# A second order for every queue of a gated recurrence and gated linear unit kernel

## The chip, the core and the metric

The kernel runs on one core of one Trainium2 chip. The metric is the device time of one execution in microseconds, as the median over several runs. A profile is one execution of its own: it has a span, from the first to the last instruction, and a time a little longer than the span.

## The reference

The inputs are `x`, `r_gate` and `i_gate`, each 4 x 6336 x 256 in fp32, a vector `a_param` of 256, two 256 x 256 matrices and the weights of a causal convolution with five taps per channel.

```python
a_base = sigmoid(a_param)
a_t  = exp(8 * sigmoid(r_gate) * log(clip(a_base)))
norm = sqrt(max(1 - a_t * a_t, 1e-6))
u    = norm * sigmoid(i_gate) * x
h[t] = a_t[t] * h[t-1] + u[t]              # y = all h, per batch and channel
gate = sigmoid(causal_conv5(y, conv_w))    # depthwise
out  = (gate * (y @ w_val)) @ w_out
```

## The kernel before

The 4 x 6336 rows are laid end to end and cut into 51 windows of 512 rows, but for windows 0, 1 and 50, which have 256. A window is the unit of loads, gates, convolutions, products and stores. Windows are put together to 28 chunks: chunks 0, 1 and 2 are windows 0, 1 and 2, chunks 3 to 25 have two windows each, chunks 26 and 27 are windows 49 and 50. A chunk is the unit of squares, of the norm, and of the scan along time, whose result each next scan of the same half of channels needs. Twelve batches of chunks share one square root each (`BATCHES`), and one or two chunks share an exponential (`GROUPS`).

There is no scheduler at work: the kernel is under manual scheduling, and one string, `ORDER`, holds every step as a word. A loop goes through the words and emits each step's instructions, so the string fixes the order of the instructions on every engine and on the DMA queue. A word has the form `name.index.index@banks`: `cv.5@0,1` is the convolution of window 5 into PSUM banks 0 and 1; `sc.3.1` is the scan of chunk 3 for the second half of the channels. Each engine takes its own steps in the order of the string, and semaphores make a step wait for its inputs, and for whoever still reads the buffer or the PSUM bank that it writes.

The steps, with engine and line:

| word | engine | what it does | line |
|---|---|---|---|
| `lr` `li` `lx` | SP queue | load a window of r, i, x (512 KB each) | L274 |
| `st` | SP queue | store a window | L493 |
| `th` | ACT | tanh of half of r and i, for the two sigmoids | L289 |
| `pp` `up` | POOL | 1 + tanh; its product with x | L297, L309 |
| `xp` `uv` | PE, DVE | the same product for six windows, with x copied into PSUM by PE | L314, L323 |
| `tr` `ex` | PE, ACT | transpose the r gate into PSUM; exponential to a | L334, L350 |
| `sq` or `sa` | POOL or ACT | square of a | L358, L366 |
| `rt` | ACT | square root for the norm, in its own function table | L377 |
| `nt` `xg` | PE, DVE | transpose the norm; multiply it into u | L392, L399 |
| `xt` `sc` | PE, DVE | transpose u; scan along time | L408, L430 |
| `cv` `tg` | PE, ACT | convolution by five taps; tanh of its half | L442, L449 |
| `vl` `gv` | PE, DVE | product with `w_val`; gate times value | L457, L462 |
| `ou` | PE | product with `w_out` | L472 |
| `cd` or `ca` | DVE or ACT | copy the output from PSUM | L480, L482 |

The table of ACT functions is switched (L509) whenever a word needs the other table: `rt` has one, `th`, `tg` and `ex` share another. Squares and copies use no table of their own, so they can stand between. `s_small`, `s_ident`, `s_kt`, `s_diag`, `s_wl` and `s_wcast` set up constants and weights.

Buffers are rings that are shared by windows: four windows of r and i (`NRI`), four of x (`NX`), three of gates (`NTRI`), three of conv gates (`NTG`), four of outputs (`NOSB`). A load of window w + 4 can start when the gate step of window w has read its slot, and the SP queue, being in order, holds all that stands behind a load or store that waits. All eight PSUM banks are one tile, and each PE step names the banks that it writes.

Of the kernel before, what the change touches and what calls it, by code (L numbers as in the profile page):

```python
# [42 lines left out]
gv.0 ou.0.0@4 cd.0.0 st.0 sc.4.1 lx.15 cv.3@6,7 th.12 li.16 li.18 tr.7.1@4,5 tg.2 vl.2@2,3 gv.2 tg.3 ex.7.1 sq.6.1
sq.6.0 lx.14 pp.14 pp.12 up.12 tr.7.0@6,7 ex.7.0 sq.7.0 lx.16 cv.4@2,3 tg.4 th.15 ou.2.0@4,5 cd.2.0 sc.4.0 st.2 lr.18
lr.16 vl.3@6,7 xp.13@2,3 vl.4@4,5 gv.4 sq.7.1 rt.4 uv.13 th.16 sq.8.1 sq.8.0 pp.15 up.15 li.17 lr.17 up.14 ou.4.0@4,5
li.19 cv.5@0,1 lr.19 gv.3 cd.4.0 lx.17 tg.5 ou.3.0@6,7 lx.18 st.4 cd.3.0 st.3 nt.5@4,5 li.20 xg.5 pp.16 up.16 th.17
pp.17 lr.20 nt.7@6,7 xg.7 lx.19 li.21 nt.6@2,3 xg.6 th.18 pp.18 lr.21 xt.5@4,5 sc.5.1 up.17 vl.5@6,7 cv.6@0,1 tg.6
th.19 tr.9.1@2,3 ex.9.1 li.22 lr.22 up.18 sq.9.1 pp.19 gv.5 sc.5.0 tr.9.0@6,7 ex.9.0 lx.20 ou.5.0@0,1 cd.5.0 sq.10.1
xt.6@5,4 up.19 sc.6.1 cv.7@0,1 tg.7 cv.8@2,3 th.20 lr.24 tg.8 sc.6.0 vl.6@6,7 gv.6 xt.7@0,1 cv.9@4,5 ou.6.0@6,7 sc.7.0
th.21 tg.9 cd.6.0 vl.7@2,3 gv.7 vl.9@6,7 th.22 tr.11.0@0 sc.7.1 ou.7.0@2,3 vl.8@4,5 sq.9.0 tr.12.0@1 gv.9 ou.9.0@6,7  # L50
gv.8 ou.8.0@4,5 sq.10.0 st.5 cd.7.0 cd.9.0 lx.22 st.6 rt.5 lx.21 nt.8@6,7 lr.23 li.23 cd.8.0 nt.9@4,5 pp.22 pp.21
up.22 pp.20 up.20 up.21 xg.8 ex.12.0 xg.9 ex.11.0 li.24 st.7 st.9 li.25 lr.25 lx.23 lx.24 li.26 lr.26 th.23 xt.8@6,7
sc.8.0 sq.11.0 pp.23 sq.12.0 lr.27 li.27 cv.11@2,3 tg.11 cv.10@4,5 sc.8.1 cv.12@0,1 st.8 th.24 pp.24 tg.10 tg.12
vl.11@2,3 tr.11.1@6 ex.11.1 gv.11 vl.10@4,5 gv.10 th.25 xt.9@0,1 sc.9.0 tr.12.1@2 ex.12.1 ou.11.0@6,7 cd.11.0
# [24 lines left out]
lx.42 up.42 st.30 cv.33@0,1 li.45 vl.33@4,5 tg.33 st.32 gv.33 nt.21@6,7 th.44 nt.20@0,1 xg.20 lx.45 lr.47 li.48 lr.48
th.46 pp.44 xg.21 nt.22@2,3 xg.22 lx.44 cv.35@4,5 th.45 pp.45 pp.46 up.45 st.31 li.47 ou.33.0@0,1 ca.33.0 tg.35  # L80
xt.20@6,7 sc.20.0 tr.23.1@2,3 ex.23.1 sc.20.1 cv.34@0,1 tg.34 cv.36@4,5 sq.24.1 tg.36 vl.35@2,3 gv.35 vl.36@0,1 gv.36
tr.23.0@6,7 vl.34@2,3 gv.34 ou.35.0@4,5 cd.35.0 lx.46 st.33 up.44 xt.21@0,1 sq.23.1 th.48 pp.48 ex.23.0 sq.24.0
sc.21.0 sc.21.1 th.47 cv.38@2,3 tg.38 ou.36.0@4,5 ou.34.0@6,7 ca.36.0 sq.23.0 ca.34.0 xt.22@2,3 tr.25.0@0 ex.25.0
sc.22.1 sq.25.0 tr.25.1@4 ex.25.1 sc.22.0 cv.37@6,7 tg.37 cv.39@0,1 tg.39 vl.40@4,5 vl.38@6,7 gv.38 sq.25.1 rt.10
st.35 li.49 st.36 vl.37@0,1 st.34 vl.39@2,3 lx.49 lr.49 lr.50 lx.48 gv.37 ou.38.0@6,7 cd.38.0 st.38 gv.39 cv.40@0,1
ou.37.0@6,7 cd.37.0 st.37 lx.47 nt.23@2,3 nt.24@6,7 tg.40 up.46 th.49 ou.39.0@0,1 ca.39.0 xg.23 xt.23@2,3 xg.24
cv.41@6,7 gv.40 ou.40.0@0,1 tg.41 ca.40.0 pp.49 pp.47 sc.23.1 cv.42@4,5 vl.41@0,1 sc.23.0 tg.42 gv.41 tr.26.0@3 li.50
ex.26.0 vl.42@6,7 st.39 up.47 th.50 xt.24@4,5 nt.25@2,3 gv.42 up.48 xg.25 st.40 ou.41.0@0,1 ca.41.0 st.41 cv.43@6,7
tg.43 vl.43@0,1 tr.27.0@2 tr.26.1@3 ex.26.1 ex.27.0 sc.24.0 gv.43 sc.24.1 ou.42.0@6,7 sa.27.0 ca.42.0 lx.50 st.42
xt.25@4,3 sc.25.0 tr.27.1@2 sq.26.1 ex.27.1 ou.43.0@0,1 ca.43.0 sq.27.1 st.43 cv.44@6,7 tg.44 sc.25.1 cv.45@0,1 tg.45  # L90
# [450 lines left out]
```

## Time and profile before

| what | value |
|---|---|
| median of three runs | 302.48 us (301.65, 302.48, 303.43) |
| profiled execution, its time | 300.32 us |
| its span | 298.5 us |
| what lies around the span | 1.8 us |
| granted clock of TensorE, mean | 0.977 |
| busy: ACT, DVE, PE, POOL | 278.8, 247.6, 246.4, 232.8 us |
| DMA | 104.75 MB, mean 351 GB/s |

Busy time is the union of an engine's instructions. A row of a group of instructions gives the mean duration of one; neighbours on an engine overlap by some 0.1 us, so the spacing of two instructions is a little less than their duration. These are the rows of the groups that the text below uses (duration of one, largest form): gate tanh 1.918 us, exponential of 2048 columns 2.075, conv tanh 1.036, root of 6144 columns 5.329, table load 1.283, copy on ACT 1.020 and on DVE 1.210, scan of 1024 steps 2.335, gate times value 1.209, square on POOL 1.896, product with x on POOL 2.157 after 1.045 for its sum.

### The profile page before, as it was taken

The page shows a single profiled execution, that of the slowest core. Times are in us where ns is not written, and L with a number is a line of the kernel's source. Part 1 is how long each engine was busy: PE and PEld are TensorE (multiplying, and loading weights), DVE is VectorE, ACT ScalarE, POOL GpSimd, SP SyncE. Part 2 cuts the span into 40 slices and gives each one's busy share as a digit, 9 for nine tenths or more (in the row PEclk, how much of TensorE's full clock was granted, in tenths as well). Part 3 has the DMA queues.
Part 4 walks back from the last instruction along what each step waited for, and adds up shares of the span by engine and source line. Part 5 has one row for each costly group of instructions (what it writes and reads, how often), then busy time and mean ns, then how long its engine had stood idle before and what let it go on. Part 6 is the DMA issues. An engine that isn't in the chain of part 4 may idle for free.

```text
span 298.5 us, 6286 instructions
## 1 busy us (share of the span) xinstructions
PE 246.4 (83%) x2509; PEld 167.8 (56%) x2509; DVE 247.6 (83%) x206; ACT 278.8 (93%) x197; POOL 232.8 (78%) x155
## 2 busy tenths in 40 slices
PE   0374577897888598989898899998979999899993
PEld 0134255454556466757664758567647675666662
DVE  2030288849999889999999999999999899899993
ACT  6799999999999999999999999999999999969863
POOL 1478958989999899899999879998995996255300
PEclk9997599999999979999999999999999999999999
DMA  6999999999999999999999998999999977726046
GB/s 252 408 408 385 379 411 407 406 414 406 337 379 370 419 416 415 411 406 321 417 411 375 388 417 335 396 353 361 349 409 419 408 278 270 273 116 248 29 186 246
DMA packets 29995, 104.75 MB, mean 351 GB/s; under 512 B 3335, under 2 KB 3854, under 8 KB 29966
## 3 DMA queue, kind: packets, MB, share of 16 engines
q1 hardware_dynamic: 29952, 104.35, 90.5%
q8 instruction: 19, 0.31, 0.4%
q14 instruction: 10, 0.08, 0.1%
q10 hardware_dynamic: 14, 0.01, 0.0%
HBM read 78.39 MB, written 25.95 MB: 350 GB/s over the span
## 4 chain that ended last, share of the span: by engine, by line
ACT 31%; PE 23%; DVE 13%; issue 13%; DMA 12%; POOL 5%; SPq 1%; ACTq 0%; DVEq 0%; POOLq 0%
ACT tring L289 10%; ACT aring L350 8%; DMA riring<-in_r_gate_dram 7%; DVE yring L430 7%; PE banks L442 5%; ACT tgring L449 5%; PE banks L457 5%; ACT ering L377 4%; PE banks L472 4%; PE banks L392 3%; DMA riring<-in_i_gate_dram 3%; DVE tgring L462 3%; DVE oring L480 2%; DMA xring<-in_x_dram 2%; ACT L509 2%
## 5 line engine op out<-in xcount | busy, mean ns | idle before, releaser
L430 DVE TENSOR_TENSOR_SCAN yring<-aring,yring,banks 128x1024 bf16<-128x1024 f32 (+5 forms) x54 | 106.2, 1988 | 0.9 <-PE banks L408 0.6
L358 POOL TENSOR_TENSOR ering<-aring 128x1024 f32<-128x1024 f32 (+2 forms) x54 | 91.5, 1713 | 9.7 <-ACT aring L350 9.7
L309 POOL TENSOR_TENSOR uring<-tring,xring 128x1024 bf16<-128x1024 bf16 (+1 forms) x45 | 94.6, 2113 | 4.9 <-DMA xring<-in_x_dram 3.5
L289 ACT ACTIVATE tring<-riring 128x2048 bf16<-128x2048 f32 (+1 forms) x51 | 93.8, 1867 | 4.1 <-DMA riring<-in_i_gate_dram 1.9
L297 POOL TENSOR_SCALAR tring<-tring 128x1024 bf16<-128x1024 bf16 (+1 forms) x45 | 45.8, 1026 | 30.5 <-ACT tring L289 30.4
L442 PE MATMUL banks<-yring,diag 64*64 64x512 bf16 (+7 forms) x1080 | 61.9, 361 | 4.6 <-ACT aring L350 1.6
L462 DVE SCALAR_TENSOR_TENSOR tgring<-tgring,banks 128x1024 bf16<-128x1024 bf16 (+1 forms) x51 | 58.9, 1178 | 5.5 <-PE banks L457 4.4
L472 PE MATMUL banks<-wo,tgring 128*128 128x256 bf16 x396 | 51.4, 274 | 4.7 <-DVE tgring L462 3.5
L350 ACT ACTIVATE aring<-banks,khf 128x2048 f32<-128x2048 bf16 (+3 forms) x38 | 54.1, 1474 | 0.5 <-PE banks L334 0.4
L449 ACT ACTIVATE tgring<-banks 128x1024 bf16<-128x1024 f32 (+1 forms) x51 | 50.4, 1009 | 3.4 <-PE banks L442 3.3
L457 PE MATMUL banks<-yring,wv 128*128 128x512 bf16 (+4 forms) x216 | 49.4, 361 | 5.0 <-DVE oring L480 2.2
L472 PEld LDWEIGHTS <-tgring 128*128 128x128 bf16 x396 | 41.0, 114 | 15.7 <-DVE tgring L462 9.6
L442 PEld LDWEIGHTS <-diag 64*64 64x64 bf16 x1080 | 30.3, 106 | 28.8 <-issue 13.6
L377 ACT ACTIVATE ering<-ering 128x4096 bf16<-128x4096 f32 (+5 forms) x15 | 44.9, 3019 | 0.1
L399 DVE TENSOR_TENSOR uring<-banks,uring 128x2048 bf16<-128x2048 bf16 (+2 forms) x28 | 29.8, 1095 | 18.2 <-PE banks L392 17.9
L480 DVE COPY oring<-banks 128x1024 f32<-128x1024 f32 (+1 forms) x35 | 40.6, 1181 | 4.8 <-ACT aring L350 2.4
L334 PE MATMUL banks<-ident_b,tring 128*128 128x128 bf16 x396 | 29.0, 227 | 12.2 <-ACT tring L289 10.4
L334 PEld LDWEIGHTS <-tring 128*128 128x128 bf16 x396 | 25.1, 101 | 17.7 <-ACT tring L289 11.7
L457 PEld LDWEIGHTS <-wv 128*128 128x128 bf16 x216 | 19.7, 97 | 26.3 <-issue 12.4
L392 PE MATMUL banks<-ident,ering 128*128 128x128 f32 x198 | 28.8, 296 | 6.8 <-DVE oring L480 2.6
L392 PEld LDWEIGHTS banks<-ident,ering 128*128 128x128 f32 x198 | 25.9, 208 | 13.5 <-ACT ering L377 7.7
L408 PE MATMUL banks<-ident,uring 128*128 128x128 f32 x198 | 27.5, 282 | 2.6 <-DVE uring L399 2.5
(36 smaller groups left out, 113.1 us busy)
## 6 DMA issues: line engine op xcount, KB each, us to landing
riring<-in_i_gate_dram SPq DMA_DIRECT2D x48, 512.0 KB, 8.2
riring<-in_r_gate_dram SPq DMA_DIRECT2D x48, 512.0 KB, 8.3
xring<-in_x_dram SPq DMA_DIRECT2D x48, 512.0 KB, 8.0
out_dram<-oring SPq DMA_DIRECT2D x48, 512.0 KB, 5.7
riring<-in_r_gate_dram SPq DMA_DIRECT2D x3, 256.0 KB, 6.3
riring<-in_i_gate_dram SPq DMA_DIRECT2D x3, 256.0 KB, 6.5
xring<-in_x_dram SPq DMA_DIRECT2D x3, 256.0 KB, 5.3
out_dram<-oring SPq DMA_DIRECT2D x3, 256.0 KB, 7.3
```

What stands on the lines that cost most here:

```text
L289: nc.scalar.activation(out=tring[:, w % NTRI, a:a + 2, 0:J, :], in_=riring[:, w % NRI, :, 0:J, :], func=ACT.Tanh, scale=0.5)
L309: nc.gpsimd.tensor_tensor(out=u, in0=t1, in1=xt, op=ALU.mult)
L350: nc.scalar.activation(out=dst, in_=src, func=ACT.Exp, scale=khf[:, h:h + 1], bias=khf[:, h:h + 1])
L358: nc.gpsimd.tensor_tensor(out=e, in0=a, in1=a, op=ALU.mult)
L377: nc.scalar.activation(out=ering[:].bitcast(BF16)[:, 4 * o:4 * o + 2 * n], in_=ering[:, 2 * o:2 * o + 2 * n], func=ACT.Sqrt, scale=-0.25, ...
L392: nc.tensor.transpose(out=bank[:, k:k + P], in_=ering[:, e + q:e + wins[w] // 2:nq], identity=ident[:])
L430: nc.vector.tensor_tensor_scan(out=yring[:, h, col:col + o1 - o0], data0=aring[:, h, a_at[c] + o0:a_at[c] + o1], data1=xT[:, o0:o1], initi ...
L442: nc.tensor.matmul(out=gp[oh * 64:oh * 64 + 64, h, a:b], lhsT=diag[half * 64:half * 64 + 64, h, k, :], rhs=yring[half * 64:half * 64 + 64, ...
L449: nc.scalar.activation(out=tgring[:, w % NTG, :, 0:wins[w]], in_=live.pop(("gp", w))[:, :, 0:wins[w]], func=ACT.Tanh, scale=0.5)
L457: nc.tensor.matmul(out=val[:, m, a:b], lhsT=wv[:, hk, m * P:(m + 1) * P], rhs=yring[:, hk, col:col + b - a], start=(hk == 0), stop=(hk == ...
L462: nc.vector.scalar_tensor_tensor(out=tgring[:, w % NTG, :, 0:wins[w]], in0=tgring[:, w % NTG, :, 0:wins[w]], scalar=1.0, in1=live.pop(("va ...
L472: nc.tensor.matmul(out=ops[:, j * D:(j + 1) * D], lhsT=gv[:, hk, j:wins[w]:J], rhs=wo[:, hk, :], start=(hk == 0), stop=(hk == H - 1))
```

## The change

The string `ORDER` is replaced by another. Its words are the same steps: the same loads, windows, chunks, groups, batches, rings and matmuls. Three things differ.

- The order of all words, and with it that of every engine's queue and of the DMA queue.
- The PSUM banks: of the 248 steps that name banks in both orders, 201 name others.
- Who does some of the steps. Output copies on ACT are those of windows 11, 21, 27, 28, 34, 35 and 39 to 50 (18), before 15, 23, 29, 33, 34, 36, 39 to 43, 45 to 48 and 50 (16); the others are on DVE. Squares on ACT are chunk 0's and chunk 4's second half, before chunk 4's first half and chunk 27's first half. The windows whose product with x goes through PSUM and DVE are 3, 4, 6, 12, 14 and 15, before 1, 3, 7, 8, 9 and 13.

The first ten and the last thirteen lines of both strings (of 62 before):

```diff
 ORDER = """
-s_ident s_small s_kt s_diag li.2 lr.2 th.2 lr.3 lr.0 li.0 th.0 pp.0 tr.2.0@0 li.1 lr.1 tr.0.0@1 ex.2.0 th.1 lx.0 lx.2
-li.3 up.0 tr.2.1@2 ex.2.1 tr.0.1@0 ex.0.0 tr.1.1@3 ex.1.1 tr.1.0@4 sq.1.1 ex.0.1 sq.0.1 lx.3 xp.3@0,1 lx.1 lr.6 th.3
-sq.0.0 rt.0 lr.5 sq.2.0 pp.2 up.2 nt.0@5 xg.0 xt.0@2,3 li.5 th.5 sq.2.1 li.6 lr.4 uv.3 th.6 pp.6 pp.5 xp.1@5 sc.0.0
-sc.0.1 cv.0@2,3 uv.1 li.4 th.4 tg.0 s_wl.1 ex.1.0 lx.4 li.7 tr.3.1@0,1 s_wl.0 lr.7 ex.3.1 lx.5 tr.3.0@2,3 ex.3.0
-s_wl.3 lx.6 lx.7 pp.4 up.4 th.7 lr.9 rt.2 xp.7@2,3 li.8 uv.7 sa.4.0 sq.4.1 sq.3.1 sq.1.0 rt.1 nt.2@0 xg.2 nt.1@1 xg.1
-s_wl.2 lr.8 li.10 lx.8 xt.2@2,3 xt.1@0,1 sc.1.1 li.9 lr.10 sq.3.0 rt.3 li.11 up.6 sc.1.0 lx.10 lr.11 sc.2.1 sc.2.0
-up.5 th.8 lx.11 s_wcast th.10 lx.9 pp.10 up.10 lr.14 th.9 li.13 li.14 lr.13 xp.8@4,5 li.12 lr.12 uv.8 th.11 li.15
-nt.3@0,1 xg.3 nt.4@6,7 pp.11 up.11 cv.1@2,3 tg.1 xg.4 xt.3@0,1 sc.3.1 vl.1@4,5 tr.5.0@6,7 ex.5.0 sq.5.0 tr.5.1@2,3
-gv.1 ou.1.0@1 cd.1.0 st.1 lx.12 lr.15 ex.5.1 vl.0@4,5 xp.9@6,7 th.14 sq.5.1 cv.2@2,3 sc.3.0 th.13 uv.9 lx.13 xt.4@1,0
-gv.0 ou.0.0@4 cd.0.0 st.0 sc.4.1 lx.15 cv.3@6,7 th.12 li.16 li.18 tr.7.1@4,5 tg.2 vl.2@2,3 gv.2 tg.3 ex.7.1 sq.6.1
-...
-sc.21.0 sc.21.1 th.47 cv.38@2,3 tg.38 ou.36.0@4,5 ou.34.0@6,7 ca.36.0 sq.23.0 ca.34.0 xt.22@2,3 tr.25.0@0 ex.25.0
-sc.22.1 sq.25.0 tr.25.1@4 ex.25.1 sc.22.0 cv.37@6,7 tg.37 cv.39@0,1 tg.39 vl.40@4,5 vl.38@6,7 gv.38 sq.25.1 rt.10
-st.35 li.49 st.36 vl.37@0,1 st.34 vl.39@2,3 lx.49 lr.49 lr.50 lx.48 gv.37 ou.38.0@6,7 cd.38.0 st.38 gv.39 cv.40@0,1
-ou.37.0@6,7 cd.37.0 st.37 lx.47 nt.23@2,3 nt.24@6,7 tg.40 up.46 th.49 ou.39.0@0,1 ca.39.0 xg.23 xt.23@2,3 xg.24
-cv.41@6,7 gv.40 ou.40.0@0,1 tg.41 ca.40.0 pp.49 pp.47 sc.23.1 cv.42@4,5 vl.41@0,1 sc.23.0 tg.42 gv.41 tr.26.0@3 li.50
-ex.26.0 vl.42@6,7 st.39 up.47 th.50 xt.24@4,5 nt.25@2,3 gv.42 up.48 xg.25 st.40 ou.41.0@0,1 ca.41.0 st.41 cv.43@6,7
-tg.43 vl.43@0,1 tr.27.0@2 tr.26.1@3 ex.26.1 ex.27.0 sc.24.0 gv.43 sc.24.1 ou.42.0@6,7 sa.27.0 ca.42.0 lx.50 st.42
-xt.25@4,3 sc.25.0 tr.27.1@2 sq.26.1 ex.27.1 ou.43.0@0,1 ca.43.0 sq.27.1 st.43 cv.44@6,7 tg.44 sc.25.1 cv.45@0,1 tg.45
-cv.46@6,7 tg.46 pp.50 vl.45@0,1 gv.45 vl.46@4,5 vl.44@6,7 up.50 sq.26.0 gv.46 gv.44 rt.11 cv.48@2,3 ou.45.0@0,1
-ca.45.0 st.45 nt.26@4 nt.27@5 ou.44.0@6,7 up.49 xg.26 xg.27 cd.44.0 tg.48 st.44 xt.26@0,1 cv.47@4,5 tg.47 sc.26.0
-sc.26.1 vl.48@6,7 gv.48 ou.46.0@2,3 vl.47@4,5 gv.47 ca.46.0 st.46 cv.49@0,1 tg.49 xt.27@6,7 sc.27.0 vl.49@2,3 gv.49
-ou.47.0@4,5 sc.27.1 ca.47.0 st.47 ou.48.0@0,1 ca.48.0 st.48 ou.49.0@2,3 cd.49.0 st.49 cv.50@4,5 tg.50 vl.50@0,1 gv.50
-ou.50.0@0 ca.50.0 st.50
+s_ident s_small s_kt s_diag lr.2 lr.0 li.2 li.0 lr.1 th.2 th.0 tr.2.0@0 ex.2.0 li.1 pp.0 tr.2.1@1 lx.2 ex.2.1 lx.1
+lx.0 sq.2.1 tr.0.0@2 tr.0.1@3 lr.3 lx.3 li.4 li.3 lr.4 ex.0.1 ex.0.0 th.1 pp.1 sa.0.1 sq.0.0 rt.0 lr.5 li.5 nt.0@2
+sq.2.0 up.0 xg.0 xt.0@3,2 rt.2 sc.0.1 sc.0.0 up.1 pp.2 up.2 tr.1.0@1 nt.2@0 xp.3@4,5 tr.1.1@3 ex.1.0 lr.6 th.3 li.6
+th.4 cv.0@6,7 uv.3 th.5 pp.5 lx.5 lr.7 s_wl.2 lx.4 s_wl.3 s_wl.0 li.7 lx.7 th.6 ex.1.1 xg.2 xt.2@4,5 sq.1.1 up.5 tg.0
+tr.3.1@0,1 ex.3.1 sq.1.0 li.10 sq.3.1 lx.6 tr.3.0@2,3 ex.3.0 sq.3.0 lr.8 xp.4@6,7 s_wl.1 li.8 lr.10 sq.4.0 sa.4.1 uv.4
+th.7 pp.7 lr.9 up.7 lx.8 li.9 lx.9 li.11 lr.11 lx.11 s_wcast rt.1 xp.6@6,7 nt.1@2 uv.6 xg.1 xt.1@6,7 rt.3 nt.3@2,3
+sc.1.1 sc.1.0 cv.1@6,7 th.8 th.9 lx.10 lr.12 li.12 tg.1 vl.1@0,1 lr.13 sc.2.0 li.13 pp.8 xg.3 gv.1 th.10 lr.14
+vl.0@2,3 li.14 xt.3@6,7 ou.1.0@4 gv.0 ou.0.0@2 cd.0.0 cd.1.0 sc.2.1 sc.3.1 up.8 th.11 tr.5.1@0,1 ex.5.1 tr.5.0@2,3
+ex.5.0 cv.2@4,5 tg.2 st.0 st.1 lr.15 lx.12 sc.3.0 pp.10 vl.2@0,1 pp.9 up.9 th.12 pp.11 li.15 up.10 th.13 up.11 lx.15
+th.14 gv.2 nt.4@2,3 xg.4 lr.16 lx.13 cv.3@4,5 tg.3 sq.6.0 sq.5.0 ou.2.0@0,1 lr.17 cd.2.0 st.2 xt.4@2,3 cv.4@6,7 tg.4
+...
+vl.36@4,5 gv.36 cv.38@6,7 st.33 th.47 tr.25.1@2 xt.22@4,5 ca.35.0 st.35 sc.21.1 ex.25.1 sq.25.1 tr.25.0@0 tg.38
+ex.25.0 cv.37@1,2 sc.22.0 sq.25.0 tg.37 vl.38@6,7 gv.38 vl.37@0,1 gv.37 rt.10 ou.36.0@2,3 cd.36.0 li.49 lx.47 lx.46
+ou.38.0@6,7 cd.38.0 st.36 st.38 ou.37.0@0,1 cd.37.0 st.37 cv.39@2,3 cv.40@6,7 tg.39 sc.22.1 tg.40 pp.46 nt.23@0,1
+up.46 th.49 xg.23 vl.39@4,5 gv.39 pp.47 up.47 nt.24@2,3 xg.24 vl.40@6,7 gv.40 pp.48 th.50 ou.39.0@4,5 ca.39.0
+xt.23@0,1 sc.23.1 lx.50 sc.23.0 tr.26.1@2 tr.26.0@3 ex.26.1 ex.26.0 lx.48 st.39 up.48 cv.42@6,7 tg.42 cv.41@4,5 tg.41
+ou.40.0@2,3 ca.40.0 vl.41@6,7 gv.41 xt.24@4,5 tr.27.0@2 sc.24.1 sq.26.1 ex.27.0 sq.27.0 tr.27.1@3 vl.42@0,1 ex.27.1
+pp.50 st.40 ou.41.0@6,7 ca.41.0 up.50 st.41 cv.44@2,3 tg.44 cv.43@6,7 tg.43 gv.42 ou.42.0@2,3 ca.42.0 st.42 lx.49
+pp.49 sq.27.1 sq.26.0 rt.11 nt.25@0,1 vl.43@6,7 vl.44@2,3 sc.24.0 cv.45@4,5 tg.45 xg.25 xt.25@0,1 gv.44 ou.44.0@2,3
+ca.44.0 gv.43 ou.43.0@6,7 ca.43.0 sc.25.1 cv.46@4,5 nt.26@1 vl.45@2,3 tg.46 st.44 st.43 vl.46@6,7 sc.25.0 cv.47@4,5
+tg.47 up.49 xg.26 gv.46 xt.26@0,1 ou.46.0@6,7 ca.46.0 st.46 vl.47@4,5 gv.45 ou.45.0@2,3 ca.45.0 st.45 cv.48@6,7 tg.48
+sc.26.1 sc.26.0 cv.49@2,3 gv.47 nt.27@6 vl.49@4,5 vl.48@0,1 xg.27 xt.27@7,6 tg.49 gv.49 gv.48 sc.27.0 ou.47.0@2,3
+ca.47.0 st.47 ou.49.0@4,5 ca.49.0 ou.48.0@0,1 st.49 ca.48.0 st.48 sc.27.1 cv.50@6,7 vl.50@4,5 tg.50 gv.50 ou.50.0@4
+ca.50.0 st.50
 """
```

## The prediction

> **What bounds the kernel now.** I read the engines' shares first, then busy time by stretches, then the order of time of ScalarE (ACT) and TensorE (PE). Shares alone name ACT, with VectorE (DVE) and PE close.
>
> ```profile
> PE 246.4 (83%) x2509; PEld 167.8 (56%) x2509; DVE 247.6 (83%) x206; ACT 278.8 (93%) x197; POOL 232.8 (78%) x155
> ```
>
> By stretches (span, then busy time of PE, PEld, DVE, ACT, POOL, then clock and DMA) the limit changes:
>
> ```profile
> 0.00:10.00 10.00, 1.21 (x7) 0.81 (x7) 1.80 (x7) 5.63 (x6) 0.97 (x7) 1.00 0.79 290
> ...
> 50.00:100.00 50.00, 42.24 (x413) 27.02 (x409) 43.41 (x34) 49.70 (x31) 48.47 (x29) 1.00 1.01 389
> 100.00:150.00 50.00, 43.97 (x483) 32.41 (x485) 46.68 (x38) 49.38 (x33) 47.82 (x29) 0.97 1.02 399
> 150.00:200.00 50.00, 46.69 (x509) 32.19 (x502) 49.21 (x39) 49.88 (x31) 46.22 (x28) 1.00 0.99 383
> 200.00:240.00 40.00, 35.67 (x389) 25.17 (x390) 38.87 (x32) 39.94 (x29) 34.75 (x22) 1.00 0.99 380
> ...
> 260.00:270.00 10.00, 10.00 (x106) 6.54 (x99) 9.95 (x8) 6.98 (x8) 5.38 (x4) 1.00 0.35 142
> 270.00:280.00 10.00, 9.87 (x117) 5.86 (x114) 10.00 (x7) 9.53 (x11) 6.51 (x6) 1.00 0.41 153
> 280.00:290.00 10.00, 10.00 (x98) 6.58 (x95) 9.19 (x12) 6.37 (x7) 0.00 (x0) 1.00 0.40 159
> ```
>
> From 50 to 240 us ACT idles 1.1 us of 190: there, time is ACT's work. From 260 us PE and DVE are full and ACT has holes. So an order can win in three ways: less ACT waiting at the start, work moved to where an engine has holes, a denser tail. ACT in order of time (start, duration, line, tile, count) shows the waits at the start (last bracket) and my two landmarks, the square roots rt.4 (68.82) and rt.10 (249.51):
>
> ```profile
> 5.58 1.91 ACT L289 ACTIVATE tring<-riring 128x2048 bf16<-128x2048 f32 x1 [0.83 <-DMA riring<-in_r_gate_dram]
> 9.22 1.06 ACT L289 ACTIVATE tring<-riring 128x1024 bf16<-128x1024 f32 x1 [1.73 <-DMA riring<-in_i_gate_dram]
> ...
> 19.57 3.71 ACT L289 ACTIVATE tring<-riring 128x2048 bf16<-128x2048 f32 x2 [0.54 <-POOL uring L309]
> ...
> 46.95 1.91 ACT L289 ACTIVATE tring<-riring 128x2048 bf16<-128x2048 f32 x1 [0.57 <-DMA riring<-in_r_gate_dram]
> ...
> 68.82 5.43 ACT L377 ACTIVATE ering<-ering 128x4096 bf16<-128x4096 f32 x2
> ...
> 249.51 5.33 ACT L377 ACTIVATE ering<-ering 128x6144 bf16<-128x6144 f32 x1
> ```
>
> **What the change moves.** Counting the order's words (a word is a step; rt.4 is the root of batch 4): the same operations, except that two output copies go from DVE to ACT (33 and 18 against 35 and 16; both more on ACT lie in the tail, windows 44 and 49). Price by rows: DVE -2 x 1.21 us, ACT +2 x 1.02. Of the six windows gated through PSUM, one of 256 rows becomes one of 512: DVE +0.7, PE +0.8, POOL -1.4, all before 60 us. The squares taken by ACT are two as before and so are the table loads, 20. All else is order.
>
> **Start, up to rt.4.** I walk ACT's new queue with the spacing of rows (gate tanh 1.83 us, conv tanh 0.95, exponential of 2048 columns 1.95, table load 1.28) and the landings of rows. Bytes moved are from the GB/s row: 1.9 MB by 7.5 us, 8.0 by 22.4, 13.7 by 37.3, 16.8 by 44.8; a transfer is usable 1 to 2 us later (x of window 3, 4.5 MB in, at 15.0). The first tanh now has r.0 ahead of its second load: 0.65 us later, 6.2. The next has i.0 fourth and not fifth, 1.6 MB in and not 2.1: its 1.73 us go. Roots 0 and 2 now share one table switch, as 2, 1 and 3 did; root 2's last square ends 2.3 us after window 1's tanh (POOL 0.62 + 0.61 + 1.04), and ACT covers this with a square, a load and root 0 (0.4 + 1.3 + 0.6). By then window 2's gate product is done, so the 0.54 goes too. What stays is DMA: window 6 (7.9 MB) is usable at 23.3 to 24.1 and wanted at 23.0, window 9 (15.2 MB) at 42.2 to 43 and wanted at 41.5, window 11 (16.8 MB) at 46.1 to 47, as before. So window 11's tanh starts near 46.5 against 46.95, with conv tanh 1 already done, and when window 14's is over (some 58.8 against the last of that three at 58.9) conv tanh 2 is done as well. Lead in ACT work: 1.5 us if DMA is at its late end, 2.2 at its early end; I take 1.7, near the late end, since landings of this trace are the nearer row.
>
> **Middle, rt.4 to rt.10.** ACT's rows between neighbouring roots, with 5% off for the overlap of neighbours, give 29.3, 30.1, 32.2, 29.5, 27.1, 32.8 us for the order before; the roots stand 29.3, 30.5, 32.0, 29.5, 27.0, 32.4 apart. So here time is ACT's sum, and DVE and POOL may run over it in one interval (32.1, 36.2) without showing. The new order has 29.5, 30.9, 25.7, 36.0, 26.3, 30.9. DVE's running sum gets ahead of ACT's by at most 2.0 us (before 2.8), POOL's falls behind (before 5.9 ahead), and loads, at 0.4 MB/us, run at most 8.2 us ahead of ACT (before 9.3): no new debt at this grain. Waits inside an interval it cannot show; I take 1.1 us, as before, and bound it by 0.4 (the share of 150 to 240 us) and 5.9 (the idle time of its first 50 us). Before rt.10 one conv tanh fewer and one small square more are done, -0.6. So rt.10 starts 1.7 + 0.6 = 2.3 us sooner, 247.2.
>
> **Tail.** After rt.10 the new order leaves ACT 40.1 us of rows (37.4 before), DVE 42.7 (42.7: the two copies leave, scan 22.1 moves behind), PE 44.1 (42.0). Before, PE's first transposes after rt.10 and its last convolution stand here:
>
> ```profile
> 254.89 2.19 PE L392 MATMUL banks<-ident,ering 128*128 128x128 f32 x16 [0.89 <-ACT ering L377]
> ...
> 292.14 0.74 PE L442 MATMUL banks<-yring,diag 64*64 64x256 bf16 x20
> ```
>
> That is 37.3 us for 35.8 of rows. The new order has 37.5 between the same two steps. PE is the later of the engines: walked by rows from the table switch ahead of rt.10, copy 44 frees its banks at 30.0 us where PE wants them at 31.3, scan 25.0 gives convolution 47 its input at 32.6 where PE gets there at 33.0, copy 45 frees its banks at 38.2 for 38.5, and conv tanh 48 at 39.4 for 39.7. At no idle the last convolution comes 0.3 us later from rt.10, at the old 1.5 us of idle 1.7. I take 0.9, nearer the dense end, because the walk finds little to wait for. After the last scan the chain is the same. Late loads do no harm here: x.48 is issued when copy 37 is over, some 7 us after rt.10's switch begins; 8.0 us to land and 2.2 + 5.1 us of POOL put root 11's last square at 23, and ACT gets to that switch at 24.
>
> **Sum.** -2.3 + 0.9 = -1.4 us: span 298.5 to 297.1, the execution 300.32 to 298.9. That execution is 2.2 under the median of the runs, 302.48, so the forecast is 301.1.
>
> **A rule weighed.** The old trace shows PE at half clock in mid-kernel after a short gap:
>
> ```profile
> 103.52 3.02 PE L392 MATMUL banks<-ident,ering 128*128 128x128 f32 x16 [2.27 <-DVE oring L480]
> ```
>
> and in the stretch around them (0.77 is the clock):
>
> ```profile
> 104.50:111.90 7.40, 7.40 (x81) 5.13 (x80) 6.48 (x8) 6.85 (x6) 7.40 (x5) 0.77 1.02 415
> ```
>
> These 16 transposes took 3.02 us, the same 16 at 254.89 took 2.19, and the eight after them 1.83 against 1.04: 1.6 us of PE. The Trainium skill ("TensorE: Matmul & The Clock Gate", Part 1) has the clock halve after an idle window of about 3.4 us; this trace shows it after 2.27 us, so its threshold is not safe here. By its figure the sum stands, since no gap in the new tail nears 3.4.
>
> **Rivals.**
> - *Lead lost in the middle.* Of 248 steps that name banks in both orders, 201 name others, and PE, in order, waits for the engine that empties a bank. If ACT then waits 1.5 to 3 us more than before, -1.4 becomes about 0: 302.5. For: from 150 to 200 us PE, DVE, ACT and POOL are 92% to 100% busy. Against: the sums above.
> - *ACT starved: slower.* The same mechanism, larger: one late bank release holds PE, then the transposes for an exponential, then ACT, which has no hole to catch up in. It decides from 4.0 us of ACT idle between 50 and 240 us (1.1 + 1.4 + the 1.5 below); at 6 us the time is 306.0.
> - *Half clock in the tail.* PE is full there, so a gap of 2.3 us or more before it costs 1.6: 302.7. My largest gap is 1.2, ahead of the transposes after rt.10.
> - *A tail set by DVE.* If scan 22.1 fits in the 0.96 us that DVE waited at 256.2 and copies 44 and 49 no longer delay it, the tail gives 1 us and not costs 0.9: 299.2.
>
> **Chances.** A measurement of this kernel tells about 0.5% (1.5 us) from no change. The lead carries, 0.52 (its own range 299.3 to 302.1, from the ends above; 0.38 of it under 301.0, 0.14 over); lost in the middle 0.15; half clock 0.06; starved 0.21; DVE's tail 0.06. Faster 0.38 + 0.06 = 0.44, same 0.14 + 0.15 + 0.06 = 0.35, slower 0.21. Low end 298.6: 299.2 less most of the spread of the three runs (0.8 below the median). High end 304.6: it takes in the lost lead and the nearer part of starving.
>
> **What would show it.** Right: rt.4 near 68 with one more conv tanh done; rt.10 near 247.2; ACT idle 50 to 240 us near 1.1; PE's last convolution 43.5 us after rt.10 (42.6 before). Wrong: ACT waits on PE in the middle, a late rt.4 by loads of windows 9 to 14, or PE gaps behind root 11.

## The result and the profile after

The new order is slower by half a per cent: 302.77 us (median of 20 runs, 301.18 to 305.12) against 302.03 us for the old (20 runs), a ratio of 1.0051 [1.0029, 1.0073]. The ratio is taken over the fast runs of both kernels (one run of the old took 414.26 us) and is not the quotient of the two medians, which is 1.0025. The profiled execution took 303.86 us, with a span of 301.9 us. It is 1.1 us above its median while the one of before, 300.32, is 1.7 below its own, so by the ratio only 1.5 of the 3.4 us between the two spans belong to the kernels, and the rest to these two executions. I read the places from the profiles and the sizes from the ratios.

The shares say nothing of a loss: ACT has 1.0 us more work, with two copies more, and the others are within 1.3 us of before.

```profile
PE 246.1 (82%) x2484; PEld 169.6 (56%) x2511; DVE 247.2 (82%) x205; ACT 279.8 (93%) x199; POOL 231.5 (77%) x155
```

The busy time by those of the same stretches that the text uses, with the same columns (span, then PE, PEld, DVE, ACT, POOL, clock, DMA):

```profile
0.00:10.00 10.00, 0.75 (x5) 0.61 (x6) 1.80 (x7) 5.05 (x6) 0.97 (x7) 1.00 0.80 280
...
100.00:150.00 50.00, 42.41 (x455) 31.34 (x458) 45.84 (x37) 47.97 (x31) 45.43 (x28) 0.97 0.98 369
150.00:200.00 50.00, 43.01 (x484) 29.77 (x488) 48.52 (x37) 49.04 (x30) 45.73 (x28) 1.00 0.99 391
...
260.00:270.00 10.00, 9.95 (x107) 7.21 (x109) 9.79 (x7) 8.34 (x11) 5.07 (x6) 1.00 0.28 112
270.00:280.00 10.00, 9.95 (x111) 6.76 (x108) 9.17 (x7) 9.59 (x9) 5.03 (x5) 1.00 0.44 159
280.00:290.00 10.00, 9.95 (x115) 5.80 (x108) 9.35 (x9) 6.07 (x7) 0.85 (x1) 1.00 0.42 168
```

The first stretch, which was to be denser, has 5.05 us of ACT's work (5.63 before) and 0.75 of PE's (1.21). Between 100 and 200 us ACT lost 3.0 us, against 0.7 before. At the end PE is full, as before. ACT in order of time (start, duration, line, tile, count, wait ahead of it) tells what it waited for:

```profile
7.89 2.85 ACT L289 ACTIVATE tring<-riring 128x2048 bf16<-128x2048 f32 x2 [2.72 <-DMA riring<-in_i_gate_dram]
...
69.57 5.42 ACT L377 ACTIVATE ering<-ering 128x4096 bf16<-128x4096 f32 x2
...
111.17 1.91 ACT L289 ACTIVATE tring<-riring 128x2048 bf16<-128x2048 f32 x1 [1.82 <-DMA riring<-in_r_gate_dram]
...
151.54 1.91 ACT L289 ACTIVATE tring<-riring 128x2048 bf16<-128x2048 f32 x1 [0.85 <-DMA riring<-in_r_gate_dram]
...
250.87 5.33 ACT L377 ACTIVATE ering<-ering 128x6144 bf16<-128x6144 f32 x1
```

The first gate tanh starts at 7.89 us, not at the forecast 6.2. Root rt.4 is at 69.57 and not near 68. The tanhs of windows 23 and 31 wait for their r loads, so the two intervals around them take 32.8 and 26.6 us where 30.9 and 25.7 were forecast; the other four are within 0.4 us of theirs. Root rt.10 is at 250.87 and not at 247.2. On PE the transposes after rt.10 and the last convolution stand here:

```profile
256.25 1.23 PE L392 MATMUL banks<-ident,ering 128*128 128x128 f32 x8 [0.98 <-ACT ering L377]
...
295.35 0.74 PE L442 MATMUL banks<-yring,diag 64*64 64x256 bf16 x20
```

That is 39.1 us where before had 37.3. So three places to test: the first load, the loads of windows 23 and 31, and the tail.

For the first load, the SP queue of after and then of before (start, duration, tile, count), and the bytes that had moved shortly before the first tanh of after:

```profile
0.72 0.86 SPq L274 DMA_DIRECT2D riring<-in_r_gate_dram  x2
1.63 0.97 SPq L274 DMA_DIRECT2D riring<-in_i_gate_dram  x2
```

```profile
0.72 0.39 SPq L274 DMA_DIRECT2D riring<-in_i_gate_dram  x1
1.17 1.44 SPq L274 DMA_DIRECT2D riring<-in_r_gate_dram  x3
```

```profile
DMA packets 769, 1.93 MB, mean 247 GB/s; under 512 B 82, under 2 KB 89, under 8 KB 769
```

The i load of window 2 is issued third, at 1.63, and lands at 7.8 (that of before, issued first at 0.72, at 4.1). Window 2's two loads and r.0 ahead of the second are 1.31 MB; 1.93 MB had moved by 7.8 us. Before, 1.19 MB had moved by 5.5 us, for the 1.05 MB that the first tanh needs. So some 0.6 MB of loads that were issued later moved before the wanted one had landed: the later loads did not wait for it.

### The profile page after: what moved, and what is told of

Its sections match the earlier page's. It is cut to its first block, busy times and chain, and to the rows that moved or that the text cites. A ratio compares the mean times of both kernels' runs of the same rounds, so it can differ in the third digit from the quotient of the medians.

```text
span 301.9 us, 6254 instructions
## 1 busy us (share of the span) xinstructions
PE 246.1 (82%) x2484; PEld 169.6 (56%) x2511; DVE 247.2 (82%) x205; ACT 279.8 (93%) x199; POOL 231.5 (77%) x155
## 5 line engine op out<-in xcount | busy, mean ns | idle before, releaser
L442 PE MATMUL banks<-yring,diag 64*64 64x512 bf16 (+7 forms) x1080 | 64.1, 369 | 9.4 <-ACT oring L482 2.6
L472 PE MATMUL banks<-wo,tgring 128*128 128x256 bf16 x396 | 50.5, 273 | 6.7 <-DVE tgring L462 5.9
L457 PE MATMUL banks<-yring,wv 128*128 128x512 bf16 (+7 forms) x189 | 47.8, 360 | 4.6 <-ACT tgring L449 2.5
L472 PEld LDWEIGHTS <-tgring 128*128 128x128 bf16 x396 | 42.1, 114 | 15.2 <-DVE tgring L462 9.7
L442 PEld LDWEIGHTS <-diag 64*64 64x64 bf16 x1080 | 30.9, 107 | 33.3 <-issue 18.3
L480 DVE COPY oring<-banks 128x1024 f32<-128x1024 f32 (+1 forms) x33 | 38.1, 1181 | 1.3 <-PE banks L472 0.9
L392 PE MATMUL banks<-ident,ering 128*128 128x128 f32 x198 | 30.8, 301 | 9.6 <-ACT ering L377 6.7
L392 PEld LDWEIGHTS banks<-ident,ering 128*128 128x128 f32 x198 | 26.8, 209 | 17.3 <-ACT ering L377 10.2
```

Source lines behind the costliest of these rows:

```text
L392: nc.tensor.transpose(out=bank[:, k:k + P], in_=ering[:, e + q:e + wins[w] // 2:nq], identity=ident[:])
L442: nc.tensor.matmul(out=gp[oh * 64:oh * 64 + 64, h, a:b], lhsT=diag[half * 64:half * 64 + 64, h, k, :], rhs=yring[half * 64:half * 64 + 64, ...
L457: nc.tensor.matmul(out=val[:, m, a:b], lhsT=wv[:, hk, m * P:(m + 1) * P], rhs=yring[:, hk, col:col + b - a], start=(hk == 0), stop=(hk == ...
L472: nc.tensor.matmul(out=ops[:, j * D:(j + 1) * D], lhsT=gv[:, hk, j:wins[w]:J], rhs=wo[:, hk, :], start=(hk == 0), stop=(hk == H - 1))
```

## The experiments

The theory: the first loads' sequence makes the first tanh late, this debt brings the gate loads of windows 23 and 31 behind their tanhs, and the tail takes back what rt.10 gains. The rivals: the middle itself is worse (banks, a late release), or the tail alone makes the order slower. All runs were timed against the kernel before on the same chip. Times in the table are of one profiled execution each, in us; "idle" is ACT's between 50 and 240 us, "tail" runs from rt.10 to the last conv tanh, tg.50. Each line number of the edited kernels is one to two below that of before.

| kernel | first tanh | rt.4 | rt.9 | rt.10 | tg.50 | tail | idle | ratio to before |
|---|---|---|---|---|---|---|---|---|
| before | 5.58 | 68.8 | 217.1 | 249.5 | 292.9 | 43.4 | 1.1 | 1 |
| after | 7.89 | 69.6 | 220.3 | 250.9 | 296.3 | 45.4 | 3.2 | 1.0051 [1.0029, 1.0073] |
| e3_old_tail | 6.65 | 68.6 | 217.2 | 247.8 | 296.8 | 49.0 | 1.3 | 1.0167 [1.0119, 1.0215] |
| e4_new_tail | 5.56 | 69.0 | 217.7 | 250.4 | 295.8 | 45.4 | 2.4 | 1.0049 [1.0019, 1.0079] |
| e5_first_load | 6.08 | 68.6 | 216.7 | 247.2 | 292.7 | 45.4 | 0.7 | 0.9996 [0.9973, 1.0020] |
| e6_gate_loads | 7.40 | 69.4 | 217.8 | 248.4 | 293.8 | 45.4 | 1.1 | 0.9979 [0.9951, 1.0008] |
| e7_old_with_new_first_loads | 8.01 | 70.2 | 218.3 | 250.7 | 294.1 | 43.4 | 2.0 | 1.0017 [0.9989, 1.0045] |
| e8_both_loads | 5.66 | 68.4 | 216.9 | 247.5 | 292.9 | 45.4 | 0.9 | 0.9979 [0.9949, 1.0010] |
| e9_loads_and_old_order_from_root_9 | 5.66 | 69.0 | 218.5 | 255.4 | 298.9 | 43.4 | 6.5 | 1.0166 [1.0124, 1.0209] |
| e10_fewer_taps | 5.51 | 69.5 | 218.6 | 249.2 | 293.6 | 44.4 | 1.8 | 0.9996 [0.9966, 1.0027] |
| e11_seam_before_root_9 | 5.45 | 68.1 | 216.6 | 249.4 | 292.8 | 43.4 | 1.3 | 0.9966 [0.9935, 0.9998] |
| e12_seam_after_norm_21 | 5.67 | 69.8 | 217.6 | 252.6 | 296.1 | 43.4 | 2.8 | 1.0066 [1.0038, 1.0095] |
| e13_one_bank_choice | 5.58 | 68.5 | 216.4 | 249.8 | 293.2 | 43.4 | 1.5 | 0.9999 [0.9971, 1.0026] |

### The tails exchanged

e3 takes the new order up to just behind rt.10 and then the old order's remaining steps; e4 the old order until shortly before rt.10 and then the new order's.

```diff
 # e3_old_tail, from the new order
 ... gv.37 rt.10 ou.36.0@2,3
-cd.36.0 li.49 lx.47 lx.46 ou.38.0@6,7 ...
+pp.46 lx.46 pp.48 ca.36.0 sc.22.1 cv.39@0,1 ...
 # e4_new_tail, from the old order
 ... ca.36.0 sq.23.0 ca.34.0
-xt.22@2,3 tr.25.0@0 ex.25.0 sc.22.1 ...
+st.34 lr.50 lr.49 li.50 tr.25.1@2 xt.22@4,5 ...
```

> The new order up to the root of batch 10, then all that is left in the old order. PE's rows between the first norm transposes after that root and the last convolution go back from 37.5 to 35.7 us. Theory 'tail': the new order's loss lies in those rows, the last convolution stands 42.7 us after root 10 and not 44.5, and the time is 1.8 us under the new order's, some 0.1% under the old one's (ratio 0.999). Rival 'middle': the loss is made before root 10 (250.9 against 249.5), the tail gives back less than 0.5 us, ratio to the old kernel 1.004.

> The old order up to shortly before the root of batch 10, then all that is left in the new order. Theory 'tail': root 10 starts near 249.5 as in the old kernel, the last convolution comes 44.5 us later and not 42.6, and the time is 1.8 us over the old one's (ratio 1.006). Rival 'middle': no change that can be told from the old kernel (ratio 1.000, at most 1.002).

e3 tells nothing of the tail. The two orders do not stand at the same point behind rt.10, and the seam makes a hole of its own: PE waits 2.56 us at 254.06 for the copy of output 36, which in this splice is on ACT and behind rt.10; from 245 us on an output copy on DVE is held by its product, and PE is little busy from 250 to 260 us (first column after the span).

```profile
DVE oring L479 <- PE banks L471: 6.2, 3, 5.1
```

```profile
250.00:260.00 10.00, 6.26 (x53) 3.98 (x51) 4.50 (x5) 7.61 (x6) 1.66 (x1) 1.00 0.51 181
```

What it does show lies ahead of the seam: this is the same head as after's, and here the first tanh came at 6.65, window 23 waited 0.90 us and window 31 not at all, and rt.10 came at 247.8. The lateness of the first load differs from one execution to the next.

e4 does show the tail: with rt.10 nearly where it was before (250.4), the new tail takes 45.4 us, as in after, and the whole comes out 0.5% slower. It pays the old way to rt.10 and the new way from it.

### The loads mended

```diff
 # e5_first_load, from the new order
-lr.2 lr.0 li.2 li.0 lr.1 th.2 th.0 tr.2.0@0 ex.2.0 li.1 pp.0 ...
+li.2 lr.2 lr.0 li.0 lr.1 li.1 th.2 th.0 tr.2.0@0 ex.2.0 pp.0 ...
```

```diff
 # e6_gate_loads, from the new order
-lx.8 li.9 lx.9 ...
+li.9 lx.8 lx.9 ...
-st.7 st.6 ... lx.20 lx.22 li.25 li.23 lr.23 ...
+li.23 lr.23 st.7 st.6 ... lx.20 lx.22 li.25 ...
-li.31 pp.27 ... pp.29 lr.31 cd.16.0 ...
+li.31 lr.31 pp.27 ... pp.29 cd.16.0 ...
```

e7 gives the old order the first six loads in the new order's sequence. e8 is e5 and e6 together.

```diff
 # e7_old_with_new_first_loads, from the old order
-li.2 lr.2 th.2 lr.3 lr.0 li.0 th.0 pp.0 tr.2.0@0 li.1 lr.1 ...
+lr.2 lr.0 li.2 li.0 lr.1 li.1 th.2 lr.3 th.0 pp.0 tr.2.0@0 ...
```

```diff
 # e8_both_loads, from the new order
+ the edits of e5_first_load and e6_gate_loads
```

> The new order with only the first six loads sorted again: i of window 2 first, then r of window 2, r.0, i.0, r.1, i.1. Theory 'first load': the first gate tanh starts at 5.6 us and not 7.9, and as ACT has no holes before root 10, root 4 and root 10 come 1.5 to 2.3 us sooner; the time is 1.5 us under the new order's, level with the old one (ratio 1.000). Rival 'DMA holds it anyway': the loads of windows 6, 9 and 11 land when they did, the gain is used up by waits there, root 4 moves by under 0.5 us, ratio 1.004 to 1.005.

> The new order with four loads put earlier in the DMA queue: i and r of window 23 ahead of the stores of windows 7 and 6, r of window 31 right behind i of window 31 (before it, r of window 32, which waits for the tanh of window 28, and a store were ahead of it), i of window 9 ahead of x of window 8. Theory 'late loads': ACT's waits of 1.82, 0.85 and 0.80 us at the tanhs of windows 23, 31 and 9 go, root 10 comes some 2.5 us sooner (248.4), and the time is 1.5 to 2.5 us under the new order's (ratio to the old kernel 0.998 to 1.000). Rival 'queue full': DMA is at its rate, so other loads get later by as much and the waits move; ratio 1.004 to 1.005.

> The old order with only its first six loads in the new order's sequence: r of window 2, r.0, i of window 2, i.0, r.1, i.1. Theory 'first load': i of window 2 lands at 6.5 to 7.8 us and not at 4.1, the first gate tanh starts 1.1 to 2.3 us later, and as ACT has no holes up to root 10 the end moves by that: ratio to the old kernel 1.004 to 1.007. Rival 'the start has slack': the old order's waits at the tanhs of windows 0, 5 and 11 (1.73, 0.54, 0.57 us) take it up, ratio 1.000 to 1.002.

> The new order with both load edits: the first six loads sorted with window 2 first, and the loads of windows 9, 23 and 31 put earlier. Theory 'one cause, late loads': the two edits heal the same lead (with the first one alone the waits at windows 9, 23 and 31 were already gone), so root 10 starts within 0.7 us of 247.2, the tail is 45.4 us from root 10 to the last conv tanh, ratio 0.997 to 1.000. Rival 'two causes': the gains add, root 10 near 244.7, ratio 0.990 to 0.992.

In e5 only one load really moves in the DMA queue: li.2 goes from third place to first, and lr.2 and lr.0 one back. The loss is gone: 1.0051 becomes 0.9996, 0.55% or 1.7 us. ACT in order of time:

```profile
6.08 2.85 ACT L287 ACTIVATE tring<-riring 128x2048 bf16<-128x2048 f32 x2 [0.95 <-DMA riring<-in_r_gate_dram]
...
32.12 1.91 ACT L287 ACTIVATE tring<-riring 128x2048 bf16<-128x2048 f32 x1 [1.52 <-DVE uring L321]
...
68.56 5.42 ACT L375 ACTIVATE ering<-ering 128x4096 bf16<-128x4096 f32 x2
...
108.63 1.91 ACT L287 ACTIVATE tring<-riring 128x2048 bf16<-128x2048 f32 x1 [0.28 <-DMA riring<-in_r_gate_dram]
...
247.23 5.33 ACT L375 ACTIVATE ering<-ering 128x6144 bf16<-128x6144 f32 x1
```

The first tanh is 1.8 us earlier, rt.4 1.0 and rt.10 3.6 (1.5 to 2.3 were expected of both), and of the wait at window 23 0.28 us is left; the one at 31 is gone. By 6.0 us, 1.39 MB had moved, 1.05 of it needed. So the loads of 23 and 31, whose own words had not moved, were probably late because the order around them ran late. One execution does not show it: e10, which has the order of e5, again waits 1.08 us for the load of window 31 with its first load on time. How r.23 comes to land 2.5 us earlier when it is issued 0.7 us earlier (99.4 against 100.1) can only be argued: the stores and loads around it have shifted too.

Nor does the earlier first tanh reach rt.4 undiminished. The wait of 1.52 us at 32.12, which after does not have, is that of window 7's tanh. It writes the buffer of window 4's gates, which window 4's product on DVE still reads, and DVE waits for PE to copy x of window 4 into PSUM. That copy, in e5 and then in e8:

```profile
27.57 3.75 PE L312 MATMUL banks<-xring,ident 128*128 128x512 f32 x4 [1.08 <-DMA xring<-in_x_dram]
```

```profile
27.50 1.96 PE L312 MATMUL banks<-xring,ident 128*128 128x512 f32 x4 [1.26 <-DMA xring<-in_x_dram]
```

PE's granted clock is 0.50 in the first and 1.00 in the second. Ten executions have the new order's start. In six of them (e5, e6, e9 to e12) this copy takes 3.36 to 3.75 us and ACT waits 1.07 to 1.63 us here; in the other four (after, e3, e8, e13) it takes 1.95 or 1.96 us and ACT does not wait. What decides the clock is open: PE had been idle for 0.78 us ahead of the copy both in after and in e6. So a single execution cannot size the first load. In the seven with a first tanh at 5.5 to 6.1 us, rt.4 lies anywhere between 68.1 and 69.8.

e6 leaves the first load late (7.40) and moves those loads forward. The long waits in the middle go too, and its ratio is 0.9979. e8 has both and gains no more than e6: 0.9979, with an interval that leaves out the 0.990 to 0.992 of two gains that add up. By the ratios it is one debt, then, that either edit removes. What part of the 1.7 us falls to the start and what to the two later waits is open: the intervals of e5, e6 and e8 overlap.

e7 goes to its rival, that the old order's start has slack. The first tanh is 2.4 us late here, as expected:

```profile
8.01 2.86 ACT L288 ACTIVATE tring<-riring 128x2048 bf16<-128x2048 f32 x2 [3.27 <-DMA riring<-in_i_gate_dram]
```

yet rt.4 is 1.3 us late, rt.10 1.2, and the ratio 1.0017 cannot be told from 1. The old order had a wait of 1.73 us for i.0 right behind, which this wait now covers. (r.3 also goes back here, from third place to seventh.) So a late first load cost little where the order had waited for another load anyway.

### The tail taken apart

e9 is e8 up to shortly after rt.9, then the old order's steps; e11 has the seam 11 words earlier, shortly before rt.9; e12 33 words later. e13 is e9 with other banks for three steps, despite its name.

```diff
 # e9_loads_and_old_order_from_root_9, from e8
 ... rt.9 vl.32@0,1 gv.32 ou.32.0@0,1 cd.31.0
+cd.30.0 sc.19.0 cd.32.0 pp.43 pp.41 up.41 up.43 li.46 ...        # as in the old order, to the end
 # e11_seam_before_root_9, from e8
 ... tg.32 li.45 lr.45 lr.44 vl.31@2,3
+vl.32@4,5 gv.32 gv.31 ou.30.0@0,1 cd.30.0 xt.19@3,2 sc.19.0 ...   # as in the old order, to the end
 # e12_seam_after_norm_21, from e8
 ... gv.34 nt.21@2,3 xg.21 up.43 th.46
+pp.44 nt.22@2,3 xg.22 cv.35@4,5 pp.45 pp.46 ...                   # as in the old order, to the end
 # e13_one_bank_choice, from e9
-cv.33@0,1
+cv.33@6,7
-nt.21@6,7
+nt.21@0,1
-nt.20@0,1
+nt.20@6,7
```

> The new order with both load edits up to just after root 9, then all that is left in the old order; the seam lies where the orders have the least steps ahead of each other. PE's rows after root 10 are the old 42.1 us and not 44.1. Theory 'the tail's order': root 10 near 247 and the last conv tanh 43.4 us after it, as in the old kernel: ratio 0.990 to 0.993, a version faster than both. Rival 'PE is behind whatever the order': ACT's lead at root 10 was never PE's, PE meets root 10 with as much left to do, the last conv tanh comes 45 us or more after it, ratio 0.997 to 1.000.

> The new order with both load edits up to shortly before root 9, then the old order. The old banks of windows 31 to 33 come with it. Theory 'tail by order': the last conv tanh is 43.4 us after root 10, root 10 near 248.1 (the new order's 247.5 with 0.6 us more of ACT's work before it), ratio 0.995. Rival 'seam': a bank that is held over the seam costs PE and ACT 2 us or more, ratio 1.002 or more, with the wait seen within 10 us after the seam.

> The same with the seam later, behind the norm transposes of chunk 21 (some 13 us after root 9). Theory 'tail by order': last conv tanh 43.4 us after root 10, root 10 near 248.1, ratio 0.995. Rival 'seam': as before, ratio 1.002 or more with a wait right behind the seam.

> The kernel with both load edits and the old order from root 9, with three bank names changed near its seam: convolution 33 writes banks 6 and 7, which copy 30 frees, and not 0 and 1, which copies 31 and 30, scan 19.0 and copy 32 held for 4.6 us; the norm transposes of chunks 21 and 20 swap banks. Theory 'banks starve ACT': PE's wait of 4.56 us and ACT's of 3.91 behind it go, root 10 starts 3 to 4 us sooner (251.4 to 252.4), the last conv tanh stays 43.4 us after it, ratio to the old kernel 1.002 to 1.006. Rival 'another wait follows': the next bank is as late, root 10 moves by under 1 us, ratio 1.013 or more.

e11 has the cleanest seam. Its tail is the old one, 43.4 us, and its rt.10 is as late as the old one, 249.4 (248.1 was expected), though rt.9 is as early as in e5. tg.50 comes at 292.8, as in e5 and e8 with the new tail. In these executions the exchange of everything from rt.9 on moves the end by less than 0.2 us, and the intervals of the three ratios overlap. The two stretches from rt.9 to rt.10 and from rt.10 to tg.50, first of before, then of e5, then of e11, show why (PE's busy time is the first column after the span):

```profile
217.13:249.51 32.38, 29.23 (x337) 20.57 (x338) 31.33 (x25) 32.32 (x24) 28.39 (x19) 1.00 0.95 370
249.51:292.93 43.42, 42.10 (x437) 28.25 (x437) 40.90 (x34) 35.13 (x31) 14.52 (x11) 1.00 0.46 176
```

```profile
216.68:247.23 30.55, 27.10 (x307) 19.24 (x310) 30.16 (x25) 30.50 (x21) 25.84 (x16) 1.00 0.94 360
247.23:292.66 45.43, 43.78 (x460) 30.01 (x464) 41.28 (x33) 37.03 (x33) 17.41 (x14) 1.00 0.46 177
```

```profile
216.64:249.37 32.73, 30.27 (x342) 21.15 (x346) 32.04 (x25) 32.44 (x24) 27.97 (x18) 1.00 0.94 340
249.37:292.81 43.44, 41.88 (x434) 28.23 (x438) 40.89 (x34) 35.15 (x32) 14.52 (x11) 1.00 0.46 176
```

The new order reaches rt.10 1.8 us sooner from rt.9, because 1.9 us of ACT's rows stand behind the root and not ahead of it (32.32 to 30.50, then 35.13 to 37.03). PE has 2.1 us less ahead of it and 1.7 more behind it. From rt.9 to tg.50 the sums are 75.8 us (before), 76.0 (e5) and 76.2 (e11). The root comes earlier; the work does not.

e9 and e12 failed as tests of the tail, since each has a hole at its seam. e9's is worth a look, because it has my second rival, with something added. PE in order of time, then ACT:

```profile
226.72 2.35 PE L441 MATMUL banks<-yring,diag 64*64 64x512 bf16 x20 [4.56 <-DVE oring L479]
```

```profile
229.12 1.02 ACT L448 ACTIVATE tgring<-banks 128x1024 bf16<-128x1024 f32 x1 [3.91 <-PE banks L441]
```

Convolution 33 is to go into banks 0 and 1, which hold output 32. On DVE its copy stands behind two others and a scan, so PE waits 4.56 us and ACT, behind PE, 3.91. e13 gives the convolution banks 6 and 7 instead. The longest wait of PE in that stretch is then 1.38 us, rt.10 comes at 249.8 and not at 255.4, and the ratio falls from 1.0166 to 0.9999. So three bank names were worth 1.7%, but the banks alone are not the whole of it. Behind the gap of 4.56 us PE's granted clock is 0.50 until 230.9: convolution 33 takes 2.35 us and the next four products 1.89, where e13 has 1.27 and 1.02. And 2.1 of the 5.6 us at rt.10 were there at rt.9 already, ahead of the edit; from rt.9 to rt.10 it is 36.9 against 33.4 us. In e12 PE waits 2.21 us for DVE, a copy on ACT 2.22 us for its product (at 233.9), and rt.10 is 3.3 us later than in e11, 1.0 of it at rt.9 already.

### Less work for PE in the tail

From e5. Tap 2 of the convolution is left out for windows 41 to 47, which takes 28 of the tail's matmuls away, 1.7 us by PE's rows.

```diff
-                for k in range(CONV_K):
+                for k in ((0, 1, 3, 4) if 41 <= w <= 47 else range(CONV_K)):
```

> The new order with the first six loads sorted, and tap 2 of the convolution left out for windows 41 to 47, which takes 4 of 20 matmuls from each of seven convolutions in the tail, 1.7 us of PE by the row (1.21 us for 20). Theory 'PE sets the tail': the last conv tanh comes 43.8 us after root 10 and not 45.5, ratio to the old kernel 0.994. Rival 'a chain through DVE and ACT sets it': under 0.5 us, ratio 0.998 to 1.000.

The stretch from rt.10 to tg.50:

```profile
249.20:293.63 44.43, 42.75 (x437) 29.03 (x436) 40.99 (x33) 37.00 (x33) 17.40 (x14) 1.00 0.48 183
```

The tail is 1.0 us shorter, and so is PE's busy time: what PE was really relieved of came out in full. That lies between the theory (1.7) and the rival (under 0.5). Why PE was relieved of 1.0 us and not the 1.7 of the rows is open. The whole time cannot show it: the ratio is 0.9996, as for e5, with an interval that holds 1 us less too. This execution came to rt.10 at 249.2, 2.0 us later than e5 with the same order up to there; 1.08 us of that is the wait of window 31's tanh. In the new order these loads stand close to their due times anyway.

## Why the prediction was wrong

The direction was wrong. The forecast was 1.4 us less than before: a lead of 2.3 us at rt.10, less 0.9 in the tail. The ratio says 1.5 us more (0.51% of 302; the two medians alone say 0.7). The tail cost 2.0, so by the ratio some 0.5 us of the lead was left at rt.10. Two terms failed, then: the lead, 1.8 us too large, and the tail's cost, 1.1 too small. Together they are the 2.9 us between forecast and ratio.

- **Start, the first load: mis-sized, 1.7 us by the ratios with what follows from it.** "0.65 us later, 6.2" was 1.1 us in e3, 1.8 in e6, 2.3 in after, 2.4 in e7. I priced only the 256 KB of r.0 that now stand ahead of i.2, at 0.4 MB/us, and let the loads behind it wait for it. They do not wait: 1.93 MB had moved when 1.31 were needed. Of the rest of the start, the waits of 1.73 and 0.54 us went as forecast, but "What stays is DMA" left out the wait of window 7's tanh for window 4's product: 1.1 to 1.6 us in six of ten executions, each time with PE's clock halved, which I had weighed for the tail alone. With the first load on time, rt.4 is at 68.1 to 69.8 with one more conv tanh done; "near 68" was the best case.
- **Middle: the sums were right, the wait was not.** ACT's rows gave every interval within 0.4 us in e5. ACT's idle time was 3.15 us and not 1.1, inside the bounds of 0.4 and 5.9, and for 2.67 of it ACT waited for DMA and not for PE. I had tested loads by their running sum ("at most 8.2 us ahead of ACT, before 9.3: no new debt at this grain"); the loads of windows 23 and 31 fell late in the queue, r.23 behind two stores and four loads, which a running sum cannot show. e6 shows that earlier places are enough to mend it, e5 that an earlier first load is. That e5 has rt.10 at 247.2, the very number of the forecast, is luck: e10, with the same order up to there, has 249.2. And two errors cancel in e5: rt.4 later by some 0.6, the intervals shorter by as much in sum.
- **Tail: mis-sized, and the step before it counted as a gain.** "I take 0.9, nearer the dense end, because the walk finds little to wait for" was 2.0 to the last conv tanh, in every execution with this tail (1.85 to the last convolution in after). The walk was right that PE finds little to wait for (0.98 and 0.25 us), but idle time between its groups stays: PE was idle 1.65 us of 45.43, before 1.32 of 43.42. The upper end, the old idle time on the new rows, 1.7, was the nearer row. The cut at rt.10 misled as well. From rt.9 to tg.50 I had a gain of 1.5 us in the last interval and a loss of 0.9 behind it. A root is a landmark of ACT, and ACT is not what ends last there; over the whole stretch the orders differ by 0.2 us. The forecast for this stretch was 0.6 us less than before.

The rivals. *Half clock in the tail* did not occur: the granted clock (tenths, 40 slices of 7.5 us) dips at 30 to 45 and at 113 to 121 us, and after rt.10 only in the last slice, where PE's work ends.

```profile
PEclk9999769999999997999999999999999999999998
```

The longest gap of PE in the new tail until tg.50 is 0.98 us. The dip at 113 us lies outside the tail, and the late load of window 23 stands behind it: PE waits for a copy on ACT that follows that window's tanh.

```profile
115.13 2.30 PE L442 MATMUL banks<-yring,diag 64*64 64x512 bf16 x20 [2.33 <-ACT oring L482]
```

These 20 matmuls took 2.30 us where e13's took 1.27. So the price of the rival, half clock after a gap of 2.3 us or more, came true here, but it is no rule: PE kept its full clock after 2.56 us in e3 (at 254.06). The Trainium skill ("TensorE: Matmul & The Clock Gate", Part 1) has the clock halve after an idle window of about 3.4 us. Half clock after 4.56 us, in e9, agrees with that; half clock after 2.33 us, here, does not. *Lead lost in the middle* is what happened in part, ACT 2.1 us more idle as its condition says, but by loads and not by banks. *ACT starved by one late bank release* did not occur in after (3.15 us of idle, below the 4.0 from which it was to decide); e9 shows that the mechanism is real, and dearer than priced: 1.0166 is 5.0 us over the old order at 6.5 us of idle time, where 3.5 (306.0) was given for 6. Part of it is the half clock behind the gap. *A tail set by DVE* fell: from rt.10 to the last conv tanh DVE has 4.2 us without work in the new tail (e5), 2.5 before. Late loads in the tail did no harm that shows, as forecast.

A version that may be ahead of both came out of this. e11, the new order with its loads mended and the old order from before rt.9, has 300.72 us and a ratio of 0.9966 [0.9935, 0.9998], 1.0 us less than before. It is the best of several that lie close together (e6 and e8 have 0.9979) and was picked for it, so the third of a per cent is not safe.

## What to carry to other kernels

When several loads are issued in a burst, the one that the first instruction needs has to be issued first: price its landing by all bytes that move until then and not by those ahead of it. When a landmark on one engine comes earlier, add up what every other engine still has to do behind it, and compare two orders over a stretch that begins and ends at the same work on the engine that ends last. Before two orders are spliced, look at who holds the banks at the seam: three bank names, with the half clock behind the wait they caused, cost 1.7%, more than all else that was moved here. Profile an order more than once before you read a size from a profile: the same order came to rt.10 at 247.2 and at 249.2 us.

## What was not expected of the hardware

Of six loads issued between 0.72 and 3.1 us, the 512 KB i load of window 2 took 4.9, 5.7 and 6.2 us to land when it was issued third (e3, e6, after), and 3.3 to 3.4 us when it was first. So how late it is differs by over 1 us between executions with the same first loads. The tail, in contrast, repeats to 0.1 us: 45.4 us in five executions of kernels with the new one whole, 43.4 in six with the old (e3, whose seam lies in it, left aside). The copy of x for window 4 took 1.95 us in some executions and 3.75 in others of the same order, by the clock that PE was granted, and ACT then waited up to 1.63 us. What of the spread between executions comes from the loads and what from this clock was not tested apart.
